# A hand-scheduled attention, max-of-three and SoLU kernel: one more order for the same 2334 steps

## The chip, the core and the metric

The kernel runs on one core of one Trainium2 chip. The metric is the device time of one execution in microseconds. A profiled execution gives the trace; times without a profile stand beside it.

## What is computed

```python
# attention, B 8, H 8, S 512 rows, Ns 32 state rows, D 64, both ways
a = softmax(x @ state.T / 8);  xread = a @ state
a2 = softmax(state @ x.T / 8); sread = a2 @ x
y = concat([xread, sread], axis=2) -> (B * 544, H * D) = (4352, 512)
# max of three products, then an output matrix (768 hidden columns)
h = max(y @ w1, y @ w2, y @ w3);  y = h @ moe_w_out
# SoLU: softmax gate, layer norm, output matrix (1024 hidden columns)
h = y @ w_in;  s = h * softmax(h);  ln = (s - mean(s)) / sqrt(var(s) + 1e-6) * g_ln
out = ln @ w_out
```

The x and state arrays are float32; the weight matrices arrive as 64-bit words and are turned into float32 on the chip.

## The kernel before

Every matrix product runs on float16 pairs (a high and a low part, three products of the four). The two products with `moe_w_out` and `w_in` are folded into one matrix `Wp` (steps `aP`, `p`, `pA`, `pV`), and two groups of products use seven matrix products in place of eight (`Y`, `OP`). There are 8 batches of 512 rows (0 to 7) and one batch `s` of 256 rows that collects the sread rows of all batches.

**Steps and their names.** The whole kernel is a list of words, `ORDER`. Each word is one step, a short function of a few instructions on one engine, and the program issues the steps in the order of the list. Each engine runs its own instructions in that order, so the list fixes the queues of TensorE (PE), VectorE (DVE), ScalarE (ACT), GpSimd (POOL) and of SyncE (SP), which issues all DMAs. Between engines the framework adds semaphore waits where data or buffers need them.

The front loads and converts the weights: `L` load, `M`, `X`, `B` conversion, `Q` squares (for the w chunks a product on PE), `w..` scaling of w1 to w3, `o..` of `w_out`, `t..` the combined matrices. Then for each batch b:

- x is loaded (`xL`), scaled on all engines (`xQ xP xS xA xV`) and turned by DMA (`xT`, line 375); `cP` (line 395) multiplies it with the state; `c.`, `e.`, `n.` are the two softmaxes, `eT` another DMA turn, `rP` (line 495) the sread product.
- For each of six column blocks f, `wR` (line 276) fetches a 768 KB block of w1 to w3 from a DRAM copy into one of **two** buffers, `uP:bf` (line 884, for batch s `HP`, line 1054) multiplies it with the state, `uA uV` evict it, `hP:bf` (line 906) is the main product into three banks, `hA`, `hV`, `hW` take the maximum of the three and free one bank each.
- `j jA jG hB hG` cut h into float16 parts; `Y:bui` (line 1092, for batch 0 `zP:0t`, line 1070) is the product with `Wp` for row half u; `K`, `V` add the seven products; `zM zE zR zG zQ zH zB` are the SoLU and layer norm of one 128-row tile.
- `lS lA lV` prepare the float16 parts of `ln`, `lT:bug` (line 1228) turns one of four groups g by DMA, `OP:bui` (line 1247) multiplies with `w_out` (i 1, 2 read group 0; 4, 5 group 1; 6, 7 group 2; 3 group 3), `OA` and `OV` evict the sums, `OL` (line 1282) stores them. OP:702 reuses the bank that OA:700 reads, and OP:704 the bank that OV:701 reads.

**Buffers.** The eight PSUM banks are handed out in list order from a queue of free ones:

```python
free, held = list(range(8)), {}
def bank(name, uses=1):
    k = free.pop(0)
...
def used(t):
    h = held[id(t)]
    h[1] -= 1
    if not h[1]:
        free.append(h[0])
```

A step thus gets a bank whose last reader stands earlier in the list, and waits for that reader. The same holds for SBUF rings; the one for fetched blocks has two places (`tag="W", bufs=2`):

```python
def w_fetch(b, f):
    nc.sync.dma_start(out=Wf(b, f).rearrange("p v a i c -> p (v a i c)"), in_=W_mem[f])
...
with tc.manual_schedule():
    for word in ORDER.split():
        step(word)
```

A `wR` step waits until the product that used its place before has ended, and it stands in SP's queue behind every DMA that stands before it in the list.

## Time and profile before

| | |
|---|---|
| median of 3 runs | 785.18 us (783.29 to 785.86) |
| the profiled execution's own time | 783.33 us |
| its span, first to last instruction | 781.5 us |
| what lies around the span | 1.8 us |
| PE busy | 726.6 us, 93% |
| DVE, ACT, POOL busy | 77%, 63%, 47% |
| mean granted TensorE clock | 0.986 |

A row of the timeline is start, duration, engine, line, operation, written tile, read tiles, count, and in brackets the idle time of the engine before it with what ended it. Matmuls are pipelined: the busy time of one step can overlap the next by some tenths of a microsecond, so the distance of starts is the better length of a step.

### The profile page before, as it was taken

To read this page: it belongs to the slowest core of one execution; us is meant where nothing else is said; L and a number is where in the kernel's file an instruction comes from. 1 tells how busy PE (TensorE), PEld (TensorE's weight loads), DVE (VectorE), ACT (ScalarE), POOL (GpSimd) and SP (SyncE) were. 2 spreads that over 40 slices of the span, in tenths; PEclk is the share of its full clock that TensorE was granted. 3 is DMA by queue.
4 is the path that set the end of the run, shared out by engine and by line. 5 is a ranking of instruction groups with operands and counts; after the bars stand their busy time and mean duration, and the time that the engine had idled before them with its cause. 6 is when DMAs were issued, how large, how long until landed. Compare 5 with 4: busy or idle time off the path is not lost.

```text
span 781.5 us, 14439 instructions
## 1 busy us (share of the span) xinstructions
PE 726.6 (93%) x5547; PEld 408.7 (52%) x5547; DVE 600.0 (77%) x1179; ACT 491.6 (63%) x795; POOL 370.1 (47%) x381
## 2 busy tenths in 40 slices
...
GB/s 371 335 281 222 257 265 168 68 106 111 162 95 211 145 101 127 252 201 127 41 208 184 189 53 137 209 116 189 148 178 134 41 232 189 147 81 69 43 160 122
DMA packets 207685, 126.51 MB, mean 162 GB/s; under 512 B 181248, under 2 KB 189440, under 8 KB 207104
## 3 DMA queue, kind: packets, MB, share of 16 engines
...
HBM read 67.64 MB, written 13.63 MB: 104 GB/s over the span
## 4 chain that ended last, share of the span: by engine, by line
PE 42%; DVE 12%; DMA 6%; ACT 5%; issue 4%; POOL 2%; SPq 2%; DVEq 0%; ACTq 0%; POOLq 0%
PE h L906 13%; PE y L1092 12%; PE o L1247 10%; DMA ln<-ln 3%; DVE e L1164 2%; DVE ln L1224 2%; PE sw L884 2%; PE ys L1092 2%; DVE hm L922 1%; PE hs L1054 1%; SPq L1228 1%; DVE zb L1118 1%; ACT e L1141 1%; DVE ob L1271 1%; ACT ln L1220 1%
## 5 line engine op out<-in xcount | busy, mean ns | idle before, releaser
L906 PE MATMUL h<-A,SW 128*128 128x512 f16 x864 | 197.5, 384 | 3.5 <-DVE e L1164 2.5
L1247 PE MATMUL o<-Wo,ln 128*128 128x256 f16 x1344 | 162.0, 275 | 10.4 <-DMA ln<-ln 5.2
L1247 PEld LDWEIGHTS <-ln 128*128 128x128 f16 x1428 | 138.7, 99 | 48.5 <-issue 11.8
L906 PEld LDWEIGHTS <-SW 128*128 128x128 f16 x864 | 83.9, 99 | 105.3 <-issue 12.2
L1092 PEld LDWEIGHTS <-hT 128*128 128x128 f16 x882 | 85.5, 98 | 101.3 <-issue 4.7
L1208 POOL TENSOR_TENSOR e<-e 128x512 f32<-128x512 f32 x68 | 98.7, 1456 | 67.8 <-DVE ln L1224 37.2
L1092 PE MATMUL y<-Wp,hT 128*128 128x512 f16 x504 | 116.0, 379 | 1.3 <-DVE ob L1271 0.7
L1224 DVE TENSOR_TENSOR ln<-e,ln 128x1024 f16<-128x1024 f32 (+1 forms) x68 | 82.5, 1216 | 26.5 <-ACT ln L1220 26.4
L1092 PE MATMUL y<-Ts,hT 128*128 128x512 f16 x378 | 86.2, 379 | 0.4 <-ACT xr L412 0.4
L922 DVE SCALAR_TENSOR_TENSOR hm<-h,phi,hm 128x512 f32<-128x512 f32 x96 | 71.1, 745 | 19.7 <-ACT hm L915 13.9
L960 POOL TENSOR_TENSOR hT<-hm,hT 128x512 f16<-128x512 f32 (+1 forms) x48 | 50.6, 1058 | 75.1 <-ACT hT L956 75.1
L1220 ACT CAST ln<-e 128x1024 f16<-128x1024 f32 (+1 forms) x68 | 63.3, 934 | 31.9 <-POOL e L1208 25.4
L984 POOL TENSOR_TENSOR hT<-hs,hT 128x512 f16<-128x512 f32 x42 | 52.2, 1263 | 26.2 <-ACT hT L981 26.2
L890 ACT ACTIVATE SW<-sw 128x384 f16<-128x384 f32 x96 | 44.1, 485 | 28.0 <-PE sw L884 22.7
L894 DVE SCALAR_TENSOR_TENSOR SW<-sw,SW 128x384 f16<-128x384 f32 x96 | 51.3, 547 | 9.7 <-ACT SW L890 9.7
L1271 DVE SCALAR_TENSOR_TENSOR ob<-o,gamma,ob 128x256 f32<-128x256 f32 x80 | 37.9, 477 | 24.4 <-PE o L1247 14.7
L1186 POOL TENSOR_SCALAR rs<-rs 128x1 f32<-128x1 f32 x34 | 13.6, 400 | 89.0 <-ACT zb L1179 82.8
L1179 ACT ACTIVATE zb<-e,mean 128x1024 f32<-128x1024 f32 x30 | 34.4, 1147 | 28.8 <-DVE mean L1172 26.7
L1193 ACT ACTIVATE e<-e,nb,rs 128x1024 f32<-128x1024 f32 x34 | 42.0, 1237 | 11.1 <-POOL nb L1189 10.9
L1141 ACT ACTIVATE e<-zb,zmx,beta_x 128x1024 f32<-128x1024 f32 x28 | 34.7, 1238 | 22.0 <-DVE zmx L1132 21.4
L695 PE MATMUL wp<-Wo,Wp 128*128 128x512 f32 x96 | 46.6, 636 | 0.3 <-DVE Wo L571 0.3
L915 ACT ACTIVATE hm<-h,phi 128x512 f32<-128x512 f32 x48 | 32.7, 682 | 17.1 <-PE h L906 7.2
(211 smaller groups left out, 1115.4 us busy)
## 6 DMA issues: line engine op xcount, KB each, us to landing
...
```

Source lines behind the costliest of these rows:

```text
L695: nc.tensor.matmul(zs[f][c], a1T[f][:, e], b1[:, e, c * HALF:(c + 1) * HALF], start=e == 0, stop=e == NE - 1)
L894: nc.vector.scalar_tensor_tensor(out=sw_t[b, f][:, 1, g], in0=sw_t[b, f, g][:, :3 * P], scalar=2.0 ** -18, in1=sw_t[b, f][:, 0, g], op0=AL ...
L906: nc.tensor.matmul(parts[w], SW[:, u, g, w * P:(w + 1) * P], A[:, v, g, :], start=n == 0, stop=n == 3 * NG - 1)
L922: nc.vector.scalar_tensor_tensor(out=c, in0=h_t[b, f][i][:, :n], scalar=phi[f // 2][:, i:i + 1], in1=c, op0=ALU.mult, op1=ALU.max)
L960: nc.gpsimd.tensor_tensor(out=h_part(b, f, 1)[1], in0=src, in1=hi, op=ALU.subtract)
L984: nc.gpsimd.tensor_tensor(out=h_sum_at(b, q, 1, i), in0=hs_t[b, q][:, 2 * i:2 * i + 2], in1=h_sum_at(b, q, 0, i), op=ALU.subtract)
L1092: nc.tensor.matmul(y_t[b, u, i], h_t[b][:, v, q, j, u * P:(u + 1) * P], place(w, q), start=n == 0 and i != 3, stop=n == 3 * NQ - 1, skip_g ...
L1208: nc.gpsimd.tensor_tensor(out=half(b, u, *to), in0=half(b, u, *to), in1=half(b, u, *of), op=op)
L1220: nc.scalar.copy(o["ln", g][:, 0, 0], src)
L1224: nc.vector.tensor_tensor(out=ln[:, 0, 1], in0=l_src(b, u, g), in1=ln[:, 0, 0], op=ALU.subtract)
L1247: nc.tensor.matmul(o["bank", k][:, :OC], lT[:, v, m, :], Wo[:, x, w, m], start=n == 0 and first, stop=n == 3 * NK // 2 - 1, skip_group_che ...
L1271: nc.vector.scalar_tensor_tensor(out=o_part(b, u, *to), in0=pt[:, :OC], scalar=gamma, in1=o_part(b, u, *of), op0=ALU.mult, op1=ALU.add)
```

## The change

The 2334 words are the same before and after, each once; no step, constant, tile or pool size is altered. Only their order differs, and with it each engine's queue, SP's queue of DMAs, and which bank or ring place a step is given. Nearly every line of the list differs; this is the part that the prediction speaks of.

```diff
-L:d1 L:d0 M:d1 X:d1 L:a1 L:b0 M:d0 L:a2 X:d0 B:d1 B:d0 Q:d0 Q:d1 aP:0 aP:1 M:a1 X:a1 aA:0 B:a1 M:b0
-M:a2 X:b0 B:b0 X:a2 L:b1 aP:2 Q:a1 aA:1 M:b1 L:b2 B:a2 L:b3 aP:3 X:b1 p:00 L:w01 aP:5 Q:b0 M:b2 aP:4
-aA:4 M:b3 L:w02 B:b1 aA:3 aA:2 X:b2 p:01 B:b2 Q:b1 L:w10 X:b3 B:b3 sL Q:b2 M:w01 X:w01 M:w02 p:02
...
-oX:30 tD:1 tE:1 zG:00 tB:10 hW:10 wR:13 oB:02 zQ:00 oC:02 zP:01 tB:11 uA:120 zH:00 uA:121 qA:1
-uV:120 uV:121 xQ:2 zM:01 zE:01 X:w10 oX:31 zB:00 lA:000 uP:13 oC:21 oX:20 oB:30 hP:11 zR:01 oX:21
-oX:22 tA:1 zG:01 hA:11 qV:1 zQ:01 oC:30 lV:000 hP:12 hA:12 oX:23 zH:01 zB:01 zP:02 tV:1 hV:11 hW:11
...
-xT:41 jG:300 OP:212 OA:211 j:321 cP:4 Y:301 jA:320 jG:320 uV:400 wR:44 j:322 j:323 jA:321 jG:321
...
-V:314 uP:42 uA:420 OV:214 lA:301 lV:301 lV:300 Y:313 zM:33 lS:301 uA:421 V:313 uV:420 zE:33 hP:41
-hA:41 hV:41 lS:302 wR:43 uP:43 uA:430 uA:431 lS:303 zR:33 rP:4 uV:421 zG:33 zM:32 uV:431 lT:300
-lA:302 hW:41 hB:40 lV:302 hP:42 hA:42 xL:5 zQ:33 j:400 hV:42 hG:40 uP:44 zE:32 uV:430 hB:41 OL:211
-hG:41 j:401 j:402 xQ:5 OP:301 OA:300 hP:43 zR:32 zG:32 qA:4 uA:440 uA:441 hA:43 hV:43 zQ:32 uV:440
-OP:302 zH:33 hW:43 zB:33 wR:45 xP:5 lT:302 wR:51 uP:51 lA:303 hW:42 qV:4 OA:301 zH:32 zB:32 uP:45
-OL:210 j:403 jA:401 lV:303 lS:310 OP:306 OP:307 uA:450 hB:42 lA:311 xS:5 lT:301 j:410 j:411 OP:305
...
-zQ:42 OL:310 j:501 hB:50 hW:52 OP:406 jA:500 jG:500 j:502 zB:43 OP:407 lA:403 hB:51 xS:6 zH:42 hG:51
-j:503 uA:530 uA:531 wR:54 zB:42 xA:6 hB:52 OV:400 OV:401 uV:531 OP:405 OP:404 uP:54 uV:530 lA:410
...
-Y:602 Y:616 V:602 zM:61 qA:7 qV:7 zE:61 zR:61 V:616 zG:61 Y:603 n1:7 V:603 zM:60 Y:617 zE:60 lT:513
...
-zB:61 zB:60 V:614 zM:63 hV:s0 wR:71 lS:600 lA:600 lV:600 OV:513 lA:601 zE:63 OL:511 HP:1 hA:s1
-lV:601 uP:71 lT:600 hV:s1 Y:612 zR:63 zG:63 OP:513 Y:613 hW:s1 lS:601 hW:s0 OV:514 wR:70 lS:602
-uP:70 zQ:63 hB:s0 lA:602 uA:700 uV:700 wR:s2 lS:603 OP:601 n4:7 lV:602 wR:s3 uA:710 V:612 HP:2 hA:s2
...
-V:707 hG:75 lS:s01 Y:704 V:708 V:704 lS:s02 zM:71 OA:s00 Y:702 OP:s02 OA:611 lS:s03 lA:s02 lV:s02
-zE:71 V:702 Y:703 lT:s01 Y:716 zR:71 Y:717 lA:s03 zG:71 lV:s03 zQ:71 V:703 zM:70 Y:715 Y:714 zE:70
-zH:71 K:71 V:716 zR:70 lT:s02 zB:71 lS:700 OP:s06 zG:70 V:717 OL:610 OP:s07 zQ:70 V:718 lA:701 zH:70
-lV:701 zB:70 lA:700 V:714 lS:701 zM:73 zE:73 lV:700 lT:701 lS:703 lA:703 Y:712 OP:s05 zR:73 OV:s00
-OV:s01 zG:73 V:712 lV:703 lT:700 lT:s03 OA:s01 lS:702 zQ:73 Y:713 V:713 zM:72 OV:s02 lA:702 zE:72
-OP:s04 lT:703 OP:s03 zH:73 OV:s03 lV:702 zR:72 OP:701 OL:s01 zG:72 zB:73 lS:710 OA:700 OP:702 OP:705
-OV:s04 zQ:72 lA:711 lT:702 zH:72 lV:711 zB:72 OP:706 OL:s00 lA:710 lS:711 lS:712 OV:700 lA:712
-lV:710 lS:713 OP:707 OV:701 lT:711 OV:702 OA:701 lT:710 OP:704 OV:703 OL:701 OP:703 lV:712 OP:715
-OP:711 lT:712 OA:710 OP:712 OP:716 OV:704 OP:717 lA:713 lV:713 OL:700 OV:710 OA:711 OV:711 OV:712
-OP:714 lT:713 OV:713 OP:713 OL:711 OV:714 OL:710
+L:d0 M:d0 X:d0 L:d1 B:d0 aP:0 L:b0 Q:d0 aA:0 L:a1 M:b0 L:a2 X:b0 B:b0 L:b1 M:a1 M:d1 X:d1 X:a1 Q:b0
+L:b2 M:a2 p:00 B:a1 L:b3 Q:a1 X:o3 M:b1 aP:2 X:a2 B:d1 aP:3 B:a2 X:b1 L:w10 Q:a2 aA:2 M:b2 aA:3 B:b1
+M:b3 X:b2 Q:d1 B:b2 X:b3 sL aP:4 B:b3 aP:1 aP:5 Q:b2 Q:b3 X:w12 Q:b1 abV L:w01 L:w02 p:20123 abP
...
+oB:21 oC:12 uA:120 hV:10 tD:1 zG:00 zP:01 oB:02 oC:02 hP:11 uA:121 tE:1 tB:10 xL:2 zQ:00 xQ:2 zM:01
+zE:01 hA:11 uV:120 oX:31 oC:21 oC:30 zH:00 uV:121 hP:12 tB:11 zB:00 oX:20 zR:01 zG:01 tA:1 hW:10
+wR:14 oC:20 zQ:01 oX:21 hA:12 lA:000 hV:12 uP:13 oX:32 oX:33 oX:22 lV:000 tV:1 oB:32 zH:01 xP:2
...
+jA:320 cP:4 OV:211 cV:40 cV:41 jG:321 uA:401 uP:41 wR:43 cA:40 OP:214 jG:320 cA:41 Y:306 V:306 eV:4
+hG:35 hG:33 Y:307 eA:40 Y:302 uV:401 n0:4 eA:41 V:307 Y:305 V:302 n1:4 Y:304 lT:213 V:308 Y:317 K:31
+eW:41 Y:303 Y:316 eW:40 V:304 zM:31 n2:4 zE:31 uA:410 Y:314 uA:411 eT:4 rP:4 n3:4 n4:4 n5:4 n6:4
+zR:31 zG:31 V:303 n7:4 V:316 wR:42 OP:215 zQ:31 zM:30 zH:31 uV:411 zE:30 OV:213 V:317 hP:40 xL:5
...
+hV:41 lV:302 hP:42 lS:303 xQ:5 uA:430 hA:42 zG:33 j:400 hW:41 j:401 zQ:33 hG:40 xP:5 OP:301 jA:400
+lT:302 uP:44 uV:430 uA:431 hV:42 OL:210 zE:32 uV:431 zH:33 hW:42 zB:33 j:402 uA:440 OA:300 zR:32
+zG:32 hP:43 j:403 zQ:32 uV:440 hA:43 hV:43 uA:441 hW:43 lT:301 zH:32 OP:302 jA:401 j:410 zB:32
+OA:301 jG:400 lA:303 hB:43 OP:306 j:411 lS:310 xS:5 xA:5 OP:307 wR:51 uP:51 OV:300 jG:401 j:412
+OV:301 uP:45 OP:305 uV:441 uA:450 uV:450 j:413 hG:43 wR:50 uA:451 uV:451 lA:310 OP:304 jA:410 lV:303
...
+lT:401 j:502 hB:51 OV:400 hG:51 lA:403 uA:540 hG:50 OV:401 OP:402 uA:541 OA:401 j:510 qA:5 qV:5
+j:503 xV:6 zB:42 hP:53 hA:53 jA:501 uV:540 lA:410 hG:52 uA:550 OP:404 lS:410 wR:61 OP:405 lA:411
...
+zQ:60 Y:617 HP:0 OV:511 Y:614 V:617 V:618 zH:61 hA:s0 OV:512 hV:s0 hW:s0 zH:60 zB:61 lS:600 OP:514
+zB:60 HP:1 lA:600 lA:601 lV:600 V:614 OV:513 zM:63 zE:63 lV:601 lS:601 hA:s1 lT:513 zR:63 zG:63
+wR:71 hV:s1 uP:71 hW:s1 lT:600 OP:513 lS:602 n1:7 uA:710 Y:612 lS:603 OV:514 V:612 lA:602 OP:601
+OL:511 n2:7 lV:602 wR:70 wR:s2 uP:70 Y:613 OA:600 uA:700 zQ:63 j:s00 OP:602 n3:7 V:613 HP:2 hA:s2
...
+V:708 V:704 Y:702 Y:703 Y:711 zM:71 Y:714 V:702 lT:s00 zE:71 lS:s03 zR:71 zG:71 lA:s02 OL:610 lV:s02
+V:703 zM:70 zQ:71 zH:71 K:71 zE:70 zB:71 OP:s01 lS:700 OA:s00 zR:70 zG:70 lT:s01 zQ:70 Y:716 OP:s02
+zH:70 lA:701 V:716 OL:611 lA:s03 zB:70 lV:s03 lT:s02 lV:701 Y:717 V:717 lA:700 lS:701 Y:715 V:718
+V:714 zM:73 lV:700 Y:712 Y:713 OA:s01 V:712 zE:73 zR:73 V:713 lS:702 lA:702 lT:s03 lT:701 zG:73
+lV:702 OP:s06 lS:703 lA:703 zM:72 OP:s07 zQ:73 zE:72 lV:703 zH:73 OP:s05 zB:73 lS:710 lT:700 OV:s00
+OP:701 OV:s01 zR:72 zG:72 lT:702 OV:s02 OP:s04 lT:703 OP:s03 zQ:72 zH:72 lA:711 zB:72 OV:s03 OP:705
+OV:s04 lA:710 OL:s01 lV:711 lS:711 lS:712 OA:700 OP:706 OL:s00 lV:710 OP:707 OV:700 lA:712 OV:701
+OP:702 OA:701 OV:702 OP:704 OP:703 lT:711 OP:715 OV:703 lT:710 OP:711 lV:712 lS:713 OV:704 OL:701
+lT:712 OA:710 OP:712 lA:713 OP:716 lV:713 OP:717 OV:710 OL:700 OV:711 OP:714 OA:711 lT:713 OV:712
+OV:713 OL:711 OP:713 OV:714 OL:710
```

## Rows read from the trace of the kernel before

**Rows 1.** The page, its span and first line of part 1.

```profile
span 781.5 us, 14439 instructions
...
PE 726.6 (93%) x5547; PEld 408.7 (52%) x5547; DVE 600.0 (77%) x1179; ACT 491.6 (63%) x795; POOL 370.1 (47%) x381
```

**Rows 2.** Stretches: length, then busy PE, PEld, DVE, ACT, POOL; clock, DMA share, GB/s.

```profile
40.00:149.00 109.00, 93.06 (x737) 43.65 (x736) 100.00 (x184) 93.25 (x155) 59.85 (x58) 0.95 0.73 218
...
400.00:440.00 40.00, 34.59 (x306) 19.76 (x304) 28.86 (x56) 25.24 (x42) 19.25 (x19) 0.96 0.90 206
...
740.00:781.50 41.50, 30.84 (x241) 23.86 (x238) 21.28 (x43) 16.86 (x23) 15.49 (x14) 0.94 0.65 134
```

**Rows 3.** Waits of PE: who waited for whom, total us, times, longest us.

```profile
PE o L1247 <- DMA ln<-ln: 5.2, 7, 2.1
PE sw L884 <- DMA Wf<-wm: 4.6, 2, 2.8
PE sc L395 <- DMA xT<-xh: 4.0, 4, 1.5
```

**Rows 4.** Lengths of one step h, o, y, pr: chain of waits, start, us, what.

```profile
385.31 3.88 PE h L906 x18
389.19 1.31 PE o L1247 x12
...
397.66 1.51 PE pr L495 x48
...
449.19 1.94 PE y L1092 x9
```

**Rows 5.** Timeline of PE: hP:12, then zP:02.

```profile
148.10 5.73 PE L906 MATMUL h<-A,SW 128*128 128x512 f16 x18 [2.50 <-DVE e L1164]
153.67 6.64 PE L1070 MATMUL z<-Wp,hT 128*128 128x512 f16 x30
```

**Rows 6.** The stretch behind that wait, columns as in Rows 2.

```profile
148.30:151.70 3.40, 3.40 (x10) 1.18 (x9) 3.29 (x10) 3.40 (x7) 0.24 (x2) 0.50 0.00 0
```

**Rows 7.** Timeline of PE: uP:44, then uP:51 with uP:45.

```profile
402.98 0.68 PE L884 MATMUL sw<-Wf,sT 64*32 64x384 f16 x24
...
414.40 2.01 PE L884 MATMUL sw<-Wf,sT 64*32 64x384 f16 x48 [3.90 <-DVE p_x L293]
```

**Rows 8.** Timeline of SP: wR:45, lT:302, wR:51.

```profile
399.58 0.37 SPq L276 DMA_DIRECT2D Wf<-wm  x1
403.35 5.05 SPq L1228 DMA_TRANSPOSE ln<-ln  x1
408.45 0.57 SPq L276 DMA_DIRECT2D Wf<-wm  x1
```

**Rows 9.** Line 276, all 48 fetches, from issue to landing.

```profile
DMA to landing us min/median/max: 4.2/5.2/10.3
```

**Rows 10.** Timeline of PE: OP:405, uP:70, OP:605.

```profile
493.36 1.49 PE L1247 MATMUL o<-Wo,ln 128*128 128x256 f16 x12 [2.12 <-DMA ln<-ln]
...
637.75 0.68 PE L884 MATMUL sw<-Wf,sT 64*32 64x384 f16 x24 [1.81 <-DMA Wf<-wm]
...
652.76 1.48 PE L1247 MATMUL o<-Wo,ln 128*128 128x256 f16 x12 [1.12 <-DMA ln<-ln]
```

**Rows 11.** Timeline of PE: rP:1.

```profile
125.63 1.56 PE L495 MATMUL pr<-ah,xh 128*128 128x64 f16 x48 [1.58 <-DMA ah<-ah]
```

**Rows 12.** Timeline of PE at the end: Y:713, OP:s03, OP:702 on, OP:704 on, OP:711.

```profile
745.08 2.10 PE L1092 MATMUL y<-Wp,hT 128*128 128x512 f16 x9
...
750.44 1.48 PE L1247 MATMUL os<-Wo,ln 128*128 128x256 f16 x12 [1.95 <-DMA ln<-ln]
...
754.40 5.40 PE L1247 MATMUL o<-Wo,ln 128*128 128x256 f16 x48 [1.17 <-ACT ob L1261]
761.87 5.76 PE L1247 MATMUL o<-Wo,ln 128*128 128x256 f16 x36 [2.06 <-DVE ob L1271]
768.07 1.48 PE L1247 MATMUL o<-Wo,ln 128*128 128x256 f16 x12 [0.45 <-DMA ln<-ln]
```

More of the change, by code (lines that the diff above doesn't have):

```diff
@@ L156 @@
-hA:70 jG:s11 j:s23 wR:72 jA:s21 OV:604 jG:s21 Y:s07 lT:611 lS:613 uP:72 hV:70 Y:s05 uA:720 wR:74
-OP:611 Y:s06 uV:711 hW:70 V:s06 V:s07 lA:613 uA:721 hG:s5 V:s08 Y:s04 V:s04 zM:s1 Y:s02 Y:s03 OL:600
-uV:721 OA:610 hP:71 V:s02 OL:601 zE:s1 zR:s1 zG:s1 lV:613 hB:70 OP:612 zQ:s1 zH:s1 lS:612 uV:720
-hA:71 V:s03 uP:73 uP:74 hV:71 lA:612 zM:s0 uA:730 lV:612 hW:71 j:700 wR:75 zE:s0 lT:612 uA:731
-uV:731 j:701 hP:72 hG:70 hA:72 uV:730 hP:73 j:702 zB:s1 hV:72 hA:73 uA:740 uA:741 zR:s0 uP:75 hV:73
-uV:740 j:703 zG:s0 OP:617 hW:72 uA:750 uV:741 uA:751 OP:616 lS:s00 zQ:s0 j:710 jA:701 OV:610 OV:611
```

230 lines of the change are left out of this document (117 added, 113 removed).

## The prediction

> **What bounds the kernel now.** I read the page first: of a span of 781.5 us PE is busy 726.6 [rows 1]. Every step survives the change, so what a new order can win is in the 55 us in which PE stands still, and in what the clock loses behind such pauses. The stretches say where they lie [rows 2]. From 40 to 149 us PE is idle for 109.0 - 93.1 = 15.9 us while DVE works 100.0 of 109.0: the front is DVE's, and PE's pauses there are mostly not PE's to win. Between 149 and 740 us PE is nearly full; the largest hole is 400 to 440 us with 5.4 us. The end, from 740 us, loses 41.5 - 30.8 = 10.7 us. The waits of PE name the causes in the filled part: DMA turns ahead of OP (5.2 us), fetched blocks ahead of uP (4.6), turned x ahead of cP (4.0) [rows 3]. So I count, for each late reader, how much PE work the two lists put between the step that starts the chain and the reader: its **cover**. The lengths are 3.88 for h, 1.31 for o, 1.94 for y, 1.4 to 1.5 for pr [rows 4].
>
> A pause costs more than itself. Behind the 2.50 us in front of hP:12 the granted clock is 0.50 for a whole stretch of 3.40 us, the lower of the two levels (1.2 of 2.4 GHz), and hP:12 takes 5.73 us instead of 3.88 to 4.1 [rows 4 to 6]: 1.7 us on top.
>
> **The front, up to 149 us.** The loads start in another order (d0, d1, b0, a1 for d1, d0, a1, b0), but all eight are the same 7 MB ahead of the big product, which needs the last of them, b3; and once it runs, DVE sets the pace. I compared DVE's queue at a late milestone: ahead of zG:01 the old list has hW:10 and oC:20 that the new has not, the new has qV:1 and oC:30; everything else is common, and the four are of like size. The milestone therefore comes at the same time, within 2 us each way for a reshuffled DVE. What does change is hP:12. Two of its three banks were given back by zG:01, whose multiplications ended just before 148.10: this is its 2.50 us wait [rows 5]. In the new list zG:01 stands behind hP:12, so it cannot be the releaser; by following the queue of free banks I find hA:11, uV:120 and uV:121 instead. hA:11 is now ahead of zB:00, lA:000 and tA:1 on ACT. I credit 2.5 + 1.7 us for the pause and its slow clock, and add 0.3 for the smaller starts: **-4.5**, between -7 (DVE gains its own 2 as well) and +2 (zP:02, at 153.67, waits for DVE after all and the rest loses 2).
>
> **The fetches.** uP:51 waited 3.90 us [rows 7]. Its block takes the place of uP:44; the old list puts OP:301, hP:43, OP:302 and xP:5 between, 1.31 + 3.88 + 1.31 + 0.4 = 6.9 us of cover. SP came to wR:51 at 408.45 only, 4.9 us after uP:44 was done, since lT:302 held the queue for 5.05 us; the landing took until 414.4 [rows 7, 8]. The new list puts hP:43 and three OP between, 3.88 + 3 x 1.31 = 7.8 us. It also moves wR:51 past one more turn, lT:301. A fetch takes 4.2 us at best, 5.2 in the middle, 10.3 at worst [rows 9], so 7.8 us pays for a fetch that is issued within 2.6 us. I take half of the pause and of its clock as gone: **-2.5**, between -5.6 and +3. uP:70 waited 1.81 [rows 10] at a cover of 5.7 (uP:71, Y:612, OP:513, Y:613); now it has 5.1 (uP:71, OP:513, Y:612, OP:601): **+0.6**. Over all 48 fetches the old list has seven with less than 7 us of cover, the new has one; but uP:75 falls from 8.3 to 7.0 and uP:21 from 13.0 to 7.1: **+0.5** for these.
>
> The Trainium skill, on the page DMA: Bandwidth & Descriptors (section Anatomy of one DMA, for the gpsimd path), gives a DMA 2.0 us and its bytes at 436 GB/s. For 768 KB that is an estimate of 3.8 us, under which uP:70 would not wait at all and the sum would be 2.4 us lower; no fetch of these on SP's queue landed under 4.2 [rows 9], so the rows decide.
>
> **The turns.** OP:405 waited 2.12, OP:605 1.12 [rows 10]; OP:415 is one of the other five, 0.4 each on average [rows 3]. From the last Y of their row half to the first reader of the group, the old list has 34.7, 32.4 and 37.7 us of PE work, the new one 38.4, 36.5 and 54.5: each gains more than it lacked, **-3.6**. cP:5 has the longest of the four cP waits, 1.5 [rows 3]; between xP:5 and cP:5 the cover goes from 21.2 to 26.3: **-1.5**. Against it, rP:4 falls from 39.2 us behind cP:4 to 19.3. Its chain (two softmax steps on DVE and ACT, then a turn) is that of rP:1, which waited 1.58 [rows 11] at 17.2: **+0.7**, between 0 and 3.
>
> **The end.** After Y:713 the old PE queue holds 16 OP steps, 16 x 1.31 = 21.0 us, but OP:711, which needs the chain of the last tile, starts at 768.07, 20.9 us after Y:713 ended (745.08 + 2.10), and six steps follow [rows 12]. In between PE waits 1.95 at OP:s03, 1.17 at OP:702, 2.06 at OP:704. In the new list Y:712 and Y:713 stand together, ahead of OP:s06, s07 and s05: 19 steps, 24.9 us, are left behind Y:713. If the chain keeps its 20.9 us, the last Y and with it the end come 3 x 1.31 = 3.9 us earlier against the same total of PE work. The two hand-overs of a bank at OP:702 and OP:704 have other OP between now, so the work is there to fill the chain. **-3.5**, between -5.5 and +1.
>
> **The sum.** -4.5 - 2.5 + 0.6 + 0.5 - 3.6 - 1.5 + 0.7 - 3.5 = -13.8. Against it stand pauses that this list makes and the old had not; a cover tells who is at risk, not who is late. Outside the front's and the end's stretches the old list left PE idle for 54.9 - 15.9 - 10.7 = 28 us, part of it while the first loads came in; I give the new one a seventh of that for places that I cannot name: **+4**, between 0 and +14. Total -9.8: 783.33 - 9.8 = 773.5 for an execution like the profiled one, which was 1.85 us under the median of its runs; beside the median 785.18 that is **775.4**. A difference below 0.3%, 2.4 us, is about what a measurement of this kernel can tell from no change.
>
> **The rivals.** (1) The front keeps its time. DVE is full there, so what hP:12 no longer waits for, zP:02 waits for three steps later. The bank queue speaks against it, DVE's 100.0 of 109.0 us for it. Then the first term is nothing: 779.9.
>
> (2) The pauses move but do not shrink. The DMA queue is shared, turns, fetches and stores take each other's time, and what one reader gains another loses; the covers that grew speak against it. 785 within 2 us.
>
> (3) SP's queue turns against it, slower. The place is the fetches behind turns: wR:51 now stands behind lT:300, lT:302 and lT:301, wR:75 behind lT:612 and lT:613. If a turn holds SP as long as lT:302 did, 5.05 us [rows 8], a fetch of 5.2 [rows 9] needs 10.3 us, while eleven fetches have covers of 5.1 to 8.4, on average 7.5: 2.8 us each, and 1.7 of slow clock, 4.5. With the lost gain at uP:51 of 2.5, one hit gives 782.4, and the second decides: 786.9. With three, which I take for this case, it is 775.4 + 2.5 + 13.5 = 791.4. For it speaks that it has happened once; against it that the turns have more room too. The Trainium skill, on the same page (section Queues, rings and completion order), has each DMA engine take descriptors in the order of its ring, so that a fetch behind turns would also move its bytes after theirs. What I could see agrees: wR:51 was issued only when lT:302 had been [rows 8].
>
> **How the numbers follow.** My forecast, 769 to 782, has 0.48; rival 1, 779.9, has 0.18; rival 2 has 0.12; rival 3, 788 and more, has 0.22. Faster than 782.8: 0.48 + 0.18 + 0.01 of rival 2 = 0.67; slower than 787.5: 0.22; within: 0.11. The range leaves out 0.1 on either side: above, it reaches into rival 3, to 790; below, it takes the forecast with the unnamed pauses at nothing and the end at its best, 775.4 - 4 - 2 = 769.4, and a little of the front's: 767.
>
> **What would show it.** Right: no PE wait at hP:12 for line 1164 and no clock of 0.50 there; less than 2 us of idle at uP:51; no wait at OP:405, OP:605 and cP:5; about 25 us of PE work behind Y:713 and an end within 31 us of it. Wrong: a pause of more than 2 us at zP:02, rP:4, uP:70, uP:75 or uP:51, with 0.50 behind it, or a first 150 us that is longer. The prediction fails if the new pauses between 160 and 740 us come to more than 20 us.

## The result, and the profile after

After the change the kernel takes **764.71 us** (median, 763.28 to 766.9), before it 785.52 (783.29 to 787.28), both measured together: a ratio of **0.9739**, 95% interval 0.9702 to 0.9776. A second measurement later gave 0.974 (0.9709 to 0.977). The forecast was 775.4 and its range ended at 767: the sign was right, the size half of what came, 9.8 us forecast and 20.8 measured. The two traces lie 16.4 us apart, since before was profiled in one of its fastest executions and after in its slowest. The trace of after begins so:

```profile
span 765.1 us, 14444 instructions
...
PE 719.8 (94%) x5547; PEld 408.1 (53%) x5547; DVE 612.8 (80%) x1179; ACT 491.1 (64%) x795; POOL 362.5 (47%) x381
```

Against [rows 1] PE is busy 6.8 us less with the same 5547 instructions (mean granted clock 0.990, before 0.986), and DVE 12.8 us **more** with the same 1179; that will matter. The stretches of after, with columns as in [rows 2]; the two short ones belong to a pause shown further down:

```profile
40.00:149.00 109.00, 92.31 (x718) 43.72 (x719) 102.17 (x182) 93.00 (x155) 56.44 (x57) 0.97 0.69 210
...
176.40:179.80 3.40, 2.44 (x6) 0.89 (x7) 3.29 (x12) 2.87 (x6) 1.48 (x2) 0.52 0.02 5
179.80:183.20 3.40, 3.40 (x17) 2.38 (x16) 0.22 (x1) 3.40 (x6) 2.65 (x5) 0.50 0.00 0
202.00:695.60 493.60, 490.28 (x3983) 285.06 (x3981) 396.69 (x800) 302.52 (x496) 235.19 (x254) 1.00 0.66 154
400.00:440.00 40.00, 40.00 (x334) 22.07 (x333) 37.52 (x66) 28.04 (x50) 20.09 (x21) 1.00 0.67 142
```

The line 202.00:695.60 is the middle, from Y:101 to hP:75. Of 493.6 us PE idles 3.3; in before the same middle reads

```profile
197.00:708.00 511.00, 495.90 (x3991) 285.25 (x3991) 395.84 (x799) 304.03 (x497) 242.58 (x257) 1.00 0.63 148
```

so PE idled 15.1 us there and was busy 5.6 longer (one OP step more ahead of hP:75, 1.3 us, and about 1.7 of slow clock behind uP:51 are in it; the other 2.6 were not traced step by step). The line 400.00:440.00 is the hole of [rows 2]: full now. The waits of PE of after (who waited for whom, total us, times, longest us):

```profile
PE h L906 <- DVE SW L894: 7.7, 6, 2.9
...
PE sc L395 <- DMA xT<-xh: 2.5, 2, 2.2
...
PE o L1247 <- DMA ln<-ln: 1.3, 1, 1.3
...
PE sw L884 <- DMA Wf<-wm: 0.6, 1, 0.6
```

The three DMA waits of [rows 3] fell from 13.8 us to 4.4. At their head stands a wait that before did not have there: h for `SW` of line 894, the uV steps. The same question for the middle alone, before (197 to 708 us) and then after (202 to 695.6):

```profile
PE o L1247 <- DMA ln<-ln: 4.7, 6, 2.1
PE sw L884 <- DVE p_x L293: 3.9, 1, 3.9
PE sc L395 <- DMA xT<-xh: 2.7, 2, 1.5
PE sw L884 <- DMA Wf<-wm: 1.8, 1, 1.8
...
PE sw L884 <- DMA Wf<-wm: 0.6, 1, 0.6
...
PE hs L1054 <- DMA Wf<-wm: 0.4, 1, 0.4
```

So 13.1 of the 15.1 us that PE idled in the middle of before were waits for DMAs (the second line too: uP:51 starts at 414.40, its block landed at 414.35), and 1.0 of the 3.3 in after.

To place this I compare, at one step after another, what PE has **lost**: the start of the step less the PE work that the list puts ahead of it, each kind of step at its usual length (as in [rows 4]). In us:

| at the start of | before | after | difference |
|---|---|---|---|
| hP:00 (77 and 82 us) | 13.6 | 18.7 | +5.1 |
| zP:03 (164 us in both) | 31.4 | 30.1 | -1.3 |
| Y:101 (197 and 202 us) | 34.4 | 39.5 | +5.1 |
| hP:45 (427 and 422 us) | 46.9 | 42.5 | -4.4 |
| hP:75 (708 and 696 us) | 59.3 | 48.1 | -11.2 |
| OP:713, the last product | 68.7 | 52.3 | -16.4 |

The front lost 5 us, the middle won 16, the end won 5. The part of the front from zP:03 to Y:101, before and then after, columns as in [rows 2]:

```profile
163.78:197.00 33.22, 31.62 (x248) 17.83 (x246) 27.68 (x57) 21.38 (x39) 23.48 (x19) 1.00 0.58 125
...
163.87:202.13 38.26, 33.17 (x237) 17.56 (x235) 32.41 (x56) 20.76 (x37) 26.11 (x21) 0.91 0.49 108
```

It is 5.0 us longer in after. DVE is idle for 5.5 us of it in before and 5.9 in after, and busy for 4.7 us more. PE's timeline of after, at the places of [rows 5], [rows 7], [rows 10] and [rows 12]:

```profile
145.80 5.17 PE L906 MATMUL h<-A,SW 128*128 128x512 f16 x23
...
171.75 2.76 PE L906 MATMUL h<-A,SW 128*128 128x512 f16 x12
177.36 2.74 PE L906 MATMUL h<-A,SW 128*128 128x512 f16 x6 [2.85 <-DVE SW L894]
179.90 4.48 PE L1247 MATMUL o<-Wo,ln 128*128 128x256 f16 x24
...
414.27 1.17 PE L884 MATMUL sw<-Wf,sT 64*32 64x384 f16 x48
...
626.70 0.68 PE L884 MATMUL sw<-Wf,sT 64*32 64x384 f16 x24 [0.56 <-DMA Wf<-wm]
...
740.81 9.57 PE L1247 MATMUL o<-Wo,ln 128*128 128x256 f16 x84
751.64 1.48 PE L1247 MATMUL o<-Wo,ln 128*128 128x256 f16 x12 [1.26 <-DMA ln<-ln]
```

hP:12 (the last 18 of the 23 at 145.80) no longer waits for line 1164, as predicted; but 25 us later hP:13 stops in its middle for 2.85 us, and the two steps behind it (4.48 us for 24 instructions; two such steps take 2.8 elsewhere) run at a granted clock of 0.50 (1.2 of 2.4 GHz, the two short stretches above). The order alone does not decide the slow clock: a second trace of the same list (e16 below) has the same pause, behind it a clock of 1.00, and reaches Y:101 at 200.2 us, 1.9 earlier. From that trace the two parts behind the pause, and the stretch that follows it:

```profile
177.71 1.47 PE L906 MATMUL h<-A,SW 128*128 128x512 f16 x6 [2.85 <-DVE SW L894]
179.01 2.78 PE L1247 MATMUL o<-Wo,ln 128*128 128x256 f16 x24
...
180.20:183.60 3.40, 2.68 (x41) 1.67 (x40) 1.86 (x7) 3.40 (x7) 2.71 (x5) 1.00 0.00 0
```

uP:51 (414.27) waits for nothing, uP:70 for 0.56 in place of 1.81. At the end OP:705, 706, 707, 702, 704, 703 and 715 run in one piece of 9.57 us, where [rows 12] had 1.17 and 2.06 of waiting.

What did **not** change are the DMAs. The 48 fetches of line 276, from issue to landing, after:

```profile
DMA to landing us min/median/max: 4.2/5.3/9.2
```

and the 68 turns of line 1228:

```profile
DMA to landing us min/median/max: 3.0/4.5/9.4
```

The fetches of before are [rows 9], 4.2/5.2/10.3; its turns took 3.0/4.4/9.8. The transfers take as long as ever. Their readers stand further back, and the two late fetches are also issued sooner: wR:51 1.3 us after its place came free and wR:70 0.04, in before 4.8 and 2.0.

### The profile page after: what moved, and what is told of

Its sections match the earlier page's. It is cut to its first block, busy times and chain, and to the rows that moved or that the text cites. A ratio compares the mean times of both kernels' runs of the same rounds, so it can differ in the third digit from the quotient of the medians.

```text
span 765.1 us, 14444 instructions
## 1 busy us (share of the span) xinstructions
PE 719.8 (94%) x5547; PEld 408.1 (53%) x5547; DVE 612.8 (80%) x1179; ACT 491.1 (64%) x795; POOL 362.5 (47%) x381
## 5 line engine op out<-in xcount | busy, mean ns | idle before, releaser
L1247 PEld LDWEIGHTS <-ln 128*128 128x128 f16 x1428 | 138.9, 98 | 37.6 <-issue 9.3
L1208 POOL TENSOR_TENSOR e<-e 128x512 f32<-128x512 f32 x68 | 95.5, 1408 | 59.9 <-DVE ln L1224 33.0
L1224 DVE TENSOR_TENSOR ln<-e,ln 128x1024 f16<-128x1024 f32 (+1 forms) x68 | 86.0, 1269 | 22.3 <-ACT ln L1220 19.9
L960 POOL TENSOR_TENSOR hT<-hm,hT 128x512 f16<-128x512 f32 (+1 forms) x48 | 52.9, 1109 | 68.2 <-ACT hT L956 68.1
L890 ACT ACTIVATE SW<-sw 128x384 f16<-128x384 f32 x96 | 44.5, 484 | 24.6 <-PE sw L884 18.7
L1186 POOL TENSOR_SCALAR rs<-rs 128x1 f32<-128x1 f32 x34 | 8.9, 262 | 84.1 <-ACT zb L1179 80.5
L1118 DVE CUSTOM_DVE_ANT_0 zb<-zb,y 128x512 f32<-128x512 f32 x56 | 37.9, 680 | 9.2 <-PE y L1092 7.7
```

What stands on the lines that cost most here:

```text
L890: nc.scalar.activation(sw_t[b, f][:, 0, g], sw_t[b, f, g][:, :3 * P], AF.Copy, scale=2.0 ** -18)
L960: nc.gpsimd.tensor_tensor(out=h_part(b, f, 1)[1], in0=src, in1=hi, op=ALU.subtract)
L1208: nc.gpsimd.tensor_tensor(out=half(b, u, *to), in0=half(b, u, *to), in1=half(b, u, *of), op=op)
L1224: nc.vector.tensor_tensor(out=ln[:, 0, 1], in0=l_src(b, u, g), in1=ln[:, 0, 0], op=ALU.subtract)
L1247: nc.tensor.matmul(o["bank", k][:, :OC], lT[:, v, m, :], Wo[:, x, w, m], start=n == 0 and first, stop=n == 3 * NK // 2 - 1, skip_group_che ...
```

## The experiments

Ratios are to before, measured on the same chip, with their 95% intervals. A difference from after in microseconds compares two separate measurements, so the difference of the two ratios stands beside it.

### Which part brought what: four hybrids

"Old" and "new" are the orders of before and after. A hybrid takes one list up to a step and then the words that are left, in the other's order.

s1_oldfront (against after):

```diff
-new up to Y:101, new
+old up to Y:101, new
```

> The list of before up to the step ahead of Y:101 (197 us of its trace), then every remaining step in the order of after. My prediction priced the new front at -4.5 us: by it this hybrid is slower than after by that much, 769.2 us. The traces say the opposite: PE has lost 34.4 us of idle time and slow clock when before starts Y:101, 39.5 when after does. If these 5.1 us are the front's own doing, the hybrid is faster than after, 759.6 us. Rival: the new middle is good only because the front hands it a certain state (what is fetched, turned and evicted ahead); then the seam costs more than 5 us and the time is 765 or more.

Measured: 761.29 us, 0.9687 (0.9664 to 0.9709), and 0.9697 in a second measurement below: 3.4 us under after, 4.1 by the two ratios. The new front costs time: the prediction's first term had the wrong sign.

s2_newfront (against before):

```diff
-old up to Y:101, old
+new up to Y:101, old
```

> The list of after up to the step ahead of Y:101, then every remaining step in the order of before: the counterpart. By the prediction's term (-4.5 us) 781.0 us, by the traces (+5.1 us) 790.6 us; if front and rest are not separable, neither, and the sum of the two hybrids' differences is not that of the whole change.

Measured: 789.53 us, 1.0059 (1.0029 to 1.0089), 4.6 us slower. Both hybrids agree on the sign; 3.4 and 4.6 us are the sizes.

s3_oldtail (against after):

```diff
-new up to hP:75, new
+new up to hP:75, old
```

> The list of after up to the step ahead of hP:75 (670 us of its trace), then the rest in the order of before: Y:712 and Y:713 stand apart again, with three OP steps fewer behind Y:713. The prediction's term for the end, 3.5 us, gives 768.2 us; the difference of the traces from hP:75 to the last OP step, 5.2 us, gives 769.9; if the chain of the last tile simply takes as long as PE has work to fill it with, no change, 764.7.

Measured: 773.06 us, 0.9835 (0.9808 to 0.9862), 8.3 us over after, 7.5 by the two ratios. Part of that is the seam: the trace has a new wait of 1.5 us at OP:s01 there.

s4_newtail (against before):

```diff
-old up to hP:75, old
+old up to hP:75, new
```

> The list of before up to the step ahead of hP:75, then the rest in the order of after: only the end is new. By the prediction's term 782.0 us, by the traces 780.3 us, by the rival that the end does not depend on the order 785.5 us. Together with the first three this splits the change: front, middle (Y:101 to hP:75; the traces give it -16.3 us, the prediction's terms -5.8 and +4) and end.

Measured: 781.24 us, 0.9938 (0.9919 to 0.9958), 4.9 us faster. The end depends on the order, and gains more than the 3.5 forecast.

e16_after_again and e17_oldfront_again are after and s1 unchanged, side by side.

> The kernel after once more, unchanged, beside the next one on the same chip: 0.974, and by its trace the same pauses.

> The hybrid of before's front and after's rest once more: 0.969 if the front's 5 us are real, 0.974 if the first measurement was a lucky draw of its loads.

Measured: 763.91 us, 0.974 (0.9709 to 0.977), and 760.71 us, 0.9697 (0.967 to 0.9723). The hybrid of old front and new rest is the fastest kernel here, by 3.2 us in this pair and 3.4 in the first; the intervals overlap a little, but both measurements have the same sign and size.

### The front: why waits removed there bring nothing

e5_uv140 (against after):

```diff
-uA:140 lV:002 zP:03 tG:0 uV:131 lA:003 OA:001 lV:003 zR:02 zM:03 hB:10 uV:140 wR:15
+uA:140 uV:131 uV:140 lV:002 zP:03 tG:0 lA:003 OA:001 lV:003 zR:02 zM:03 hB:10 wR:15
```

> The list of after with two DVE steps, uV:131 and uV:140, moved ahead of lV:002. In after hP:13 stands 2.85 us still in its middle at 177.4 us: its third bank is the one that uV:140 gives back, and uV:140 stands on DVE behind lV:002 (3.15 us in that trace) and zR:02 (2.46). Two drops of the clock to 0.50 follow. Theory 'late releaser': with uV:140 early no such wait, and the pause and its slow clock, 2.85 + 1.7 = 4.5 us, come back: 760.2 us. Rival 'DVE is the bound': DVE has the same work ahead of Y:101 in whatever order, the wait moves to the next reader and the time stays at 764.7.

Measured: 765.61 us, 0.976 (0.9725 to 0.9795). In the profile hP:13 runs through; OP:005, next in the queue, then waits for the same DVE:

```profile
171.22 4.05 PE L906 MATMUL h<-A,SW 128*128 128x512 f16 x18
177.25 2.78 PE L1247 MATMUL o<-Wo,ln 128*128 128x256 f16 x24 [1.99 <-DVE e L1164]
```

That one execution reached Y:101 4.0 us before after's trace (2.1 before e16's) and took 761.92, but three of the five took 765.6 or more. No gain can be claimed; the rival fits the median.

e11_up13 (against s1) is the bank hand-over of the prediction's first term by itself:

```diff
-zB:00 lA:000 uP:13 oC:21 oX:20 oB:30 hP:11 zR:01 oX:21
-oX:22 tA:1 zG:01 hA:11 qV:1 zQ:01 oC:30 lV:000 hP:12 hA:12
+zB:00 lA:000 oC:21 oX:20 oB:30 hP:11 zR:01 oX:21
+oX:22 tA:1 hA:11 zG:01 qV:1 zQ:01 oC:30 lV:000 hP:12 uP:13 hA:12
```

> The hybrid of before's front and after's rest, with uP:13 moved behind hP:12 and hA:11 ahead of zG:01: then hP:12 gets the banks that uV:120, uV:121 and hA:11 give back, as it does in after, and not those of zG:01. This is the first term of the prediction by itself (2.5 us of wait at hP:12 and 1.7 of slow clock). If it comes back: the hybrid's 0.9687 less 0.0054, 0.963, about 757 us. Rival 'DVE is the bound of the front': zP:02, zP:03 or hP:13 wait in its place and the ratio stays 0.9687.

Measured: 761.78 us, 0.9714 (0.9684 to 0.9745): nothing gained. PE there:

```profile
141.16 6.64 PE L906 MATMUL h<-A,SW 128*128 128x512 f16 x30
150.71 1.45 PE L906 MATMUL h<-A,SW 128*128 128x512 f16 x6 [2.92 <-ACT hm L915]
...
152.71 7.94 PE L1070 MATMUL z<-Wp,hT 128*128 128x512 f16 x36
```

hP:12 starts 2.5 us earlier (the last 12 of the 30 are its own), then waits 2.92 for its third bank, hA:11's; zP:02 starts at 152.71, against 153.08 in s1, and Y:101 at 197.0 against 196.7. The wait that was taken away stands a few instructions later. It is a wait for ACT, not for DVE: hA:11 (149.98) follows right behind tA:1 there, since in e11 it still stands behind zB:00, lA:000 and tA:1, which after lists behind it. ACT in e11:

```profile
149.04 1.04 ACT L1013 CAST Ts<-t 128x1024 f16<-128x1024 f32 x1
149.98 0.68 ACT L915 ACTIVATE hm<-h,phi 128x512 f32<-128x512 f32 x1
```

So e11 shows that the hand-over alone brings nothing, and not that DVE is the reason.

e12_pool (against after) moves seven steps back in the list:

```diff
-OP:002 tF:0 uA:140 lV:002 zP:03 tG:0 uV:131
-uV:140 wR:15 wR:20 lT:001 tH:0 hP:13 tD:2 jA:100 zG:02 zE:03 OP:005 tI:0 lT:002
-hG:10 j:102 OP:006 tE:2 OV:000 uV:141 tB:20 zR:03
-hB:12 tF:1 hP:14
+OP:002 uA:140 lV:002 zP:03 uV:131
+uV:140 wR:15 wR:20 lT:001 hP:13 jA:100 zG:02 zE:03 OP:005 lT:002
+hG:10 j:102 OP:006 OV:000 uV:141 zR:03
+hB:12 tF:0 tG:0 tH:0 tI:0 tD:2 tE:2 tB:20 tF:1 hP:14
```

> The list of after with seven steps moved some 15 us later, to stand together ahead of tF:1: tF:0, tG:0, tD:2, tE:2, tB:20 on POOL, tH:0 on ACT, tI:0 on DVE. In after lV:002 takes 3.15 us on DVE beside tF:0 and tG:0, and the first small operation of zR:02, on one element per partition, 2.08 beside tD:2; over the two traces the same kind of subtraction between SBUF tiles (line 1224) takes 1.03 us on average with POOL idle and 1.52 with POOL busy all along. If POOL's steps are what lengthens them, lV:002 falls to about 1.3 us and zR:02's operation to 0.2 or less, and hP:13 waits less; if they were slow for another cause (DMA, banks), they keep 3.15 and 2.08. The whole: between 760 and 768, since the moved POOL steps then lie beside other DVE steps.

Measured: 765.31 us, 0.9759 (0.9729 to 0.9789). lV:002 and the first operation of zR:02 on DVE in after:

```profile
168.08 3.15 DVE L1224 TENSOR_TENSOR ln<-e,ln 128x1024 f16<-128x1024 f32 x1
...
172.82 2.08 DVE L1155 TENSOR_TENSOR zsm<-zsm 128x1 f32<-128x1 f32 x1
```

The three POOL steps beside them, tF:0, tG:0 and tD:2, in the same trace:

```profile
167.83 2.31 POOL L1032 TENSOR_TENSOR t<-Wp,Ts 128x1024 f32<-128x1024 f16 x1
170.22 2.13 POOL L1036 TENSOR_TENSOR t<-t 128x512 f32<-128x512 f32 x1
172.31 2.56 POOL L1002 TENSOR_TENSOR t<-Wp 128x1024 f32<-128x1024 f16 x1
```

The same two DVE operations in e12, with POOL's steps gone from beside them, and xV:2 of e12, which now meets them:

```profile
168.04 1.21 DVE L1224 TENSOR_TENSOR ln<-e,ln 128x1024 f16<-128x1024 f32 x1
...
170.74 0.15 DVE L1155 TENSOR_TENSOR zsm<-zsm 128x1 f32<-128x1 f32 x1
...
194.89 3.90 DVE L387 SCALAR_TENSOR_TENSOR xh<-xr,s_x,xh 128x1024 f16<-128x1024 f32 x2
```

3.15 became 1.21, and 2.08 became 0.15: the POOL steps beside them were the cause. hP:13 waits no more, but xV:2 takes 3.90 where after had 2.47, Y:101 comes at 201.3 (202.1 in after, 200.2 in e16) and DVE's total is 612.8, as in after. Contention was moved, not removed.

e6_mixfront and e7_seam160 put the front together from pieces:

```diff
-s1: old up to Y:101, new
+e6: old up to hP:00, new up to zP:03, old up to Y:101, new
```

```diff
-after: new
+e7: new up to zP:03, old up to Y:101, new
```

> A front of three pieces: the list of before up to hP:00, then the order of after up to zP:03, then that of before up to Y:101, then after. By the traces PE loses 13.6 us up to hP:00 in before (18.7 in after), 11.4 from there to zP:03 in after (17.8 in before), 3.0 from there to Y:101 in before (9.4 in after). If the pieces keep what they had, the front loses 28.0 us in place of the 34.4 of before: 6.4 us under the hybrid that has all of before's front (761.3), so 755 us. Rival 'DVE is the bound': both traces have done 144 us of DVE work (in before's lengths) when zP:03 starts at 163.8, so that point comes when DVE has done it; the pieces don't add up and the time is 761 to 764.

> The list of after up to zP:03, the order of before from there to Y:101, then after again. In this stretch of 35 us PE loses 9.4 us in after and 3.0 in before, and DVE works 33.7 us in after and 29.7 in before on nearly the same steps. If the loss lies in the order of this stretch (who runs beside POOL on DVE, which releaser hP:13 gets), 764.7 - 6.4 = 758.3 us. Rival: what the stretch loses is debt of the time before, and no order of it pays it: 764.7.

Measured: 761.36 us, 0.9721 (0.9692 to 0.9749), and 763.82 us, 0.9749 (0.972 to 0.9777): in both the rival's number. Both have a new pause at the seam, an OP that waits for its turn; e7's:

```profile
176.64 2.74 PE L1247 MATMUL o<-Wo,ln 128*128 128x256 f16 x12 [2.69 <-DMA ln<-ln]
```

So they don't show by themselves that DVE is the bound. But e6 is 4.8 us ahead of after at hP:00 (77.4 against 82.2 us) and only 1.0 ahead at zP:03 (162.9 against 163.9), with the same order in between and no wait at hP:12 in either: the head start does not last. The twenty traces hold only four orders up to zP:03 (old, new, e6's and e11's); it starts between 162.8 and 165.0 us in eighteen of them, and the other two, at 167.4 and 167.6, were already behind at hP:00. That DVE sets this point fits the 100.0 and 102.2 us that it is busy of the 109 from 40 to 149 us, before and after; no run isolates it.

### The middle: is the gain local?

e8_wr51 and e9_wr51_only take the pause of [rows 7] alone, against before:

```diff
-uP:44 zE:32 uV:430 hB:41 OL:211 ... zB:33 wR:45 xP:5 lT:302 wR:51 uP:51
+e8: uP:44 wR:45 wR:51 zE:32 uV:430 hB:41 OL:211 ... zB:33 xP:5 lT:302 uP:51
+e9: uP:44 zE:32 uV:430 hB:41 OL:211 ... zB:33 wR:45 wR:51 xP:5 lT:302 uP:51
```

> The list of before with wR:45 and wR:51 moved up to stand right behind uP:44, so that the fetch no longer stands behind lT:302 on SP's queue; no other word moves. Theory 'one pause, and it comes back': the 3.90 us ahead of uP:51 and 1.7 us of slow clock go, 5.6 us: ratio 0.9929 to before, about 780. The prediction's term took half of that, 2.5 us, because it held the fetch to be late in any order: then 783. Rival 'the pause moves': DVE or a turn is late next and the time is that of before within 1 us.

Measured: 782.81 us, 0.9994 (0.9969 to 1.002). uP:51 no longer waits; OP:302 does. PE in e8:

```profile
412.79 2.65 PE L1247 MATMUL o<-Wo,ln 128*128 128x256 f16 x12 [2.68 <-ACT ob L1261]
```

ACT, which OP:302 waits for (OA:300):

```profile
412.26 0.47 ACT L1261 ACTIVATE ob<-o,gamma 128x256 f32<-128x256 f32 x1 [5.02 <-DMA out_dram<-ob]
```

SP, the two fetches and then the store OL:211:

```profile
400.02 5.19 SPq L276 DMA_DIRECT2D Wf<-wm  x2
405.27 0.42 SPq L1282 DMA_DIRECT2D out_dram<-ob  x1
```

The second fetch waits at the head of SP's queue until uP:44 has ended (404.8), and the store stands behind it; OA:300 needs the buffer that the store empties, and it landed at 412.2. One word in the wrong place of SP's queue cost what the other won.

> The list of before with one word moved: wR:51 stands right behind wR:45, ahead of xP:5 and lT:302, so it can be issued when uP:44 has ended (403.7) and not after lT:302 (408.45). In the run that moved wR:45 too, OL:211 stood behind both fetches, landed at 412.2, and the pause went to OP:302 (2.7 us), whose bank OA:300 had not given back. Here OL:211 stays ahead. Theory 'SP's queue': no pause at uP:51 or OP:302, a gain of 3.9 to 5.6 us, ratio 0.993 to 0.995. The prediction's half: 2.5 us, 0.997. Rival 'moves on': lT:302 is now issued later, behind the fetch, and OP:306 waits; ratio 1.000.

Measured: 782.93 us, 0.9964 (0.9942 to 0.9987), a gain of 2.8 (1.0 to 4.5 by the interval). uP:51 waits 0.18, but the turns issued behind the fetch are late for their readers, OP:306 and OP:305:

```profile
413.42 2.79 PE L1247 MATMUL o<-Wo,ln 128*128 128x256 f16 x24 [0.75 <-DMA ln<-ln]
417.75 2.79 PE L1247 MATMUL o<-Wo,ln 128*128 128x256 f16 x24 [1.53 <-DMA ln<-ln]
```

e15_piece400, e18_piece320 and e19_middle put a piece of the new middle into before:

```diff
-old
+e15: old up to uP:42, new up to Y:414, old
+e18: old up to hP:32, new up to hP:55, old
+e19: old up to Y:101, new up to hP:75, old
```

> The list of before up to uP:42, the order of after from there to Y:414, then before again: 70 us of the middle are new, the front, the rest of the middle and the end old. PE loses 8.1 us there in before and 0.5 in the hybrid with before's front. If the middle's pauses are matters of the place (how much PE work stands between a transfer and its reader), the piece brings what it loses less, 7.6 us: ratio 0.990. Rival: as in the front the pieces don't keep their gains, the seam or a later reader takes them: 0.996 or more.

Measured: 783.02 us, 0.997 (0.9949 to 0.9991). The seam spoils it: wR:43 is issued when uP:42 has ended, and uP:43 comes next.

```profile
398.55 1.16 PE L884 MATMUL sw<-Wf,sT 64*32 64x384 f16 x24 [4.93 <-DMA Wf<-wm]
```

> As in the piece from uP:42 to Y:414, with seams where no fetch is left without work in front of its reader: the list of before up to hP:32 (326 us), the order of after from there to hP:55 (506 us), then before. In the piece tried first the seam put wR:43 behind uP:42 and uP:43 right after both, and uP:43 stood 4.93 us. PE loses 14.5 us in this stretch in before, 2.4 in the hybrid with before's front. If the middle's pauses are matters of the place, the piece brings 12 us: ratio 0.985. Rival: pieces don't keep their gains, 0.995 or more.

Measured: 775.52 us, 0.9876 (0.9849 to 0.9902): 9.7 us of the 12 expected, at the place itself. From uP:33, the last product ahead of the seam, to hP:55 the piece takes 169.8 us, before 180.7. The stretch in e18, columns as above:

```profile
326.00:496.50 170.50, 168.60 (x1441) 95.00 (x1438) 141.52 (x284) 111.76 (x181) 74.82 (x80) 1.00 0.68 166
```

> The list of before up to Y:101, the order of after from there to hP:75, before again for the end: the middle alone. The traces give the middle 16 to 18 us: ratio 0.977 to 0.980. The prediction's terms for it were -2.5, +0.6, +0.5, -3.6, -1.5, +0.7 and +4 for unnamed pauses, together -1.8: 0.998.

Measured: 768.38 us, 0.9797 (0.9766 to 0.9828): 15.9 us. In its trace PE waits 2.5 us between Y:101 and hP:75, 0.3 of it for DMAs. The middle alone brings more than three quarters of the gain. Of its pieces e18 kept most of what was expected and e15 a third (2.4 of 7.6 us); the others were not run, so that they add up is not shown.

### The end: is it Y:713?

e10_y713 and e13_tailblock, against before:

```diff
-K:71 V:716 zR:70 lT:s02 zB:71 lS:700 OP:s06 zG:70 V:717 OL:610 OP:s07 zQ:70 V:718
-lA:701 zH:70 lV:701 zB:70 lA:700 V:714 lS:701 zM:73 zE:73 lV:700 lT:701 lS:703 lA:703
-Y:712 OP:s05 zR:73 OV:s00 OV:s01 zG:73 V:712 ... zQ:73 Y:713 V:713 zM:72
+e10: ... lS:700 Y:712 Y:713 OP:s06 zG:70 V:717 OL:610 OP:s07 zQ:70 V:718 ...
+e13: ... V:714 Y:712 Y:713 OP:s06 OP:s07 lS:701 zM:73 zE:73 lV:700 V:712 ... OP:s05 zR:73 V:713 ...
```

> The list of before with two words moved: Y:712 and Y:713 stand together ahead of OP:s06; the steps of the other engines stay where they were, V:713 among them. The prediction's reason for the end: the chain of the last tile starts with Y:713, so three OP steps more behind it are worth 3.9 us, ratio 0.995 to 0.996. Rival 'DVE's place decides': V:713 still stands behind zQ:73's chain and the steps of tile 73 on DVE, so the chain starts when it did and the end keeps its time: 1.000.

Measured: 788.6 us, 1.0051 (1.0029 to 1.0074), slower by 4.0. DVE in e10 stands still until the second Y has ended, in V:718, which was listed ahead of the two Y and now stands behind them. In the program Y:713 adds into the bank of Y:715, the one that V:718 reads. Listed behind Y:713, V:718 has to wait for it and takes its product in as well: in that place this order no longer computes the same sum. Its time prices this dependency, and not the place of Y:713. DVE in e10:

```profile
745.06 0.69 DVE L1118 CUSTOM_DVE_ANT_0 zb<-zb,y 128x512 f32<-128x512 f32 x1 [5.13 <-PE y L1092]
```

> The list of before with six words moved at the end: Y:712 and Y:713, then OP:s06 and OP:s07, stand right behind V:714, V:712 behind lV:700 and V:713 behind zR:73. In the run that moved the two Y alone, V:718 (listed behind them) waited until Y:713 had ended and V:713 kept its place on DVE; here neither holds. From the end of V:713 the last tile took 29.0 us in before and 29.3 in after, so the end should come as much earlier as V:713 does: 3.9 us for the three OP steps behind Y:713 and up to 1.7 for V:713's place on DVE: ratio 0.993 to 0.996. Rival 'banks and turns': the rest of the tail's order (OP:s04, OP:s03, OP:702, OP:704) holds the end, and nothing is gained: 1.000.

Measured: 784.86 us, 1.0001 (0.9982 to 1.002). V:713 ends 3.3 us earlier after Y:701 than in before (34.3 against 37.6), but zM:72, which the chain goes on with, stands behind zG:73 and lV:703 on DVE and comes 0.3 earlier; and the two bank waits of [rows 12], at OP:702 and OP:704, are there as before:

```profile
757.80 5.40 PE L1247 MATMUL o<-Wo,ln 128*128 128x256 f16 x48 [1.38 <-ACT ob L1261]
765.27 4.09 PE L1247 MATMUL o<-Wo,ln 128*128 128x256 f16 x36 [2.07 <-DVE ob L1271]
```

Only the whole new end (s4) gains.

## Why the prediction was right and wrong

**What failed.** The time came out below the range because of the middle: -1.8 us in the sum, -15.9 measured (e19). Three of its terms were mis-sized, the half price at uP:51, the +0.6 at uP:70 and the +4 for places without a name. The front failed too, in sign, and that error went the other way and hid part of the first.

**The front (-4.5 forecast, +3.4 to +4.6 measured): the sign was wrong.** What I read was right: the bank queue (hP:12 loses its wait for zG:01) and the milestone (it was compared at zG:01, and zP:03 comes at the same time in both). Two conclusions were wrong. I credited the wait at hP:12 in full although I had called DVE full there. In after it is gone and zP:02 starts 1.8 us earlier (151.84 against 153.67), but zP:03 does not. With one OP step more ahead of it after is 1.3 us better there, and not 4.5; by then it has made up the 5.1 us that it is late at hP:00, where I had held the loads to be equal. That comes near rival 1; its mechanism, DVE, fits e6 and is not isolated, and in e11 the next late releaser was ACT. And I stopped at 149 us. From zP:03 to Y:101, which has no term of its own, PE loses 9.4 us in after and 3.0 in before. Of the 6.4 between them some 2 are the slow clock that e16 does not have. DVE is busy 32.4 us there against 27.7 with almost the same steps, because the new order lays some of them beside POOL's (3.9 us for two operations, e12). "Everything common, so the milestone comes at the same time" holds only while the steps keep their lengths. The wait at hP:13 is the same kind as the one I had followed at hP:12, a bank given back late by DVE (uV:140 stands behind lV:002 and zR:02). That the stretch costs by its contention and not by that bank alone is shown for the lengths (e12), not for the whole 5 us: no run here gave the new front its time back.

**The fetches ahead of uP:51 (-2.5) and uP:70 (+0.6): the mechanism right, the sizes wrong.** With that one fetch moved in before the gain is 2.8 us (e9), because the turns behind it become late. In after the whole pause and its slow clock are gone: between cP:4 and hP:45 PE loses 0.3 us where it lost 8.9. wR:51 was issued at 407.7, 1.3 us after uP:44 had ended and right behind lT:301, and landed 1.9 us ahead of its reader. So half of the pause was the right price for the fetch alone, and the wrong one for a place where the turns get cover too. uP:70, for which I added 0.6, waits 0.56 instead of 1.81, although its cover fell to 5.1 us: **+0.6** should have been about -1.3. The cover counts from the moment at which the place comes free and leaves out what SP adds: in before lT:600 held the queue until 631.90 and wR:70 was issued 2.0 us late, in after at once. The turns and cP:5 went as forecast: none of OP:405, OP:605, OP:415 and cP:5 waits, and rP:4 does not either, so its +0.7 was not needed.

**The unnamed pauses (+4): the largest miss of the middle.** All new pauses of the middle of after come to 2.7 us (the largest are uP:61 with 0.8 and Y:503 with 0.8). I had priced a list that is as careless as the old one at places I could not name, although the cover counts said that it is not: one fetch of 48 with under 7 us of cover in place of seven. And I gave the old list nothing for its own places without a name: of the 15.1 us that PE idled in the middle my terms name 11.0 (uP:51, uP:70, the three turns, cP:5); the other 4.1 went as well, and with them some 2.6 us of longer work. For the middle the term comes to about -4. The stretch held the ceiling: 15.1 us of idle and 4.3 of longer work at equal steps between Y:101 and hP:75.

**The end (-3.5 forecast, 4.9 measured alone, 8.3 against after): the size near, the reason not shown.** I counted three OP steps more behind Y:713, 3.9 us. That reason was not confirmed: e10 does not test it, since V:718 then waits for Y:713, and with V:712 and V:713 the two Y gained nothing (e13). The chain of the last tile goes through DVE's queue (zG:73, lV:703, zM:72) and the banks of OP:702 and OP:704, and all of these were re-ordered. From Y:701 on, zM:72 comes 4.4 us earlier in after than in before, and from there to the end of the last step on DVE it takes 26.8 us in place of 29.0. About 25 us of OP work stand behind Y:713, as I said, but the span ends 33.0 us after it, not 31. (Behind OP:711 stand five steps in before, not the six that I counted; no term uses them.) Which of the moved steps shortens the chain was not separated.

**Rivals.** Rival 2 (pauses move but do not shrink) is what happens when few words move: all of the gain is lost in e8 and e13, half of it in e9. For the whole order it is wrong: the DMAs keep their times, 5.3 us a fetch and 4.5 a turn, but their readers stand further back. Rival 3 did not occur: no fetch of the middle made PE wait over 0.6 us. The Trainium skill's page DMA: Bandwidth & Descriptors (section Anatomy of one DMA, for the gpsimd path) has the figures from which the estimate of 3.8 us a fetch was worked out, and with it uP:70 would have had 1.3 us to spare on its cover of 5.1. It still waited 0.56, and no fetch of after landed under 4.2, so the rows were the better price.

**Where the sum stands.** Front +4.6 (s2), middle -15.9 (e19), end -4.9 (s4): -16.2, against -20.8. Measured inside the new order instead, front +3.4 (s1) and end -8.3 (s3), the parts come to -20.8, by the differences of the ratios +4.1 and -7.5 to -19.3. The parts are not quite separate, because every seam between two orders makes a pause of its own. Term by term, between the two traces:

| term | forecast | traces |
|---|---|---|
| front, up to zP:03 | -4.5 | -1.3 |
| zP:03 to Y:101 | in the +4 | +6.4 |
| uP:51 (3.9 and about 1.7 of slow clock) | -2.5 | -5.6 |
| uP:70 | +0.6 | -1.3 |
| uP:75 and uP:21 | +0.5 | 0 |
| OP:405, OP:605, OP:415 | -3.6 | -3.8 |
| cP:5 | -1.5 | -1.5 |
| rP:4 | +0.7 | 0 |
| other places of the middle (what is left of its -16.3) | +4 | -4.1 |
| end | -3.5 | -5.2 |
| sum | -9.8 | -16.4 |

The +4 was written for everything outside the front and the end, so +6.4 and -4.1 fall into it together. Their +2.3 lies near it by luck: two misses that cancel.
